# Threshold attention and a bilinear FFN: the score threshold moved from GpSimd to VectorE, the last of seven products added into a free tile, and two tiles for the first batch's tails

## The chip, the cores and the metric

The kernel runs on one core of one Trainium2 chip. The time is device microseconds of one execution, and the median over several executions is what counts. Before the change 13 runs gave a median of 1550.72 us (1540.63 to 1555.79). The engines are called as the profile calls them: PE is TensorE (PEld its weight load), DVE is VectorE, ACT is ScalarE, POOL is GpSimd, SP is SyncE, which here issues nearly all DMAs.

## The reference

```python
# q, k, v: (8, 8, 576, 64); tau = 0.02
scores = matmul(q, k.transpose(0, 1, 3, 2)) / sqrt(64)
thresh = max(scores, axis=-1, keepdims=True) - tau
scores = where(scores >= thresh, scores, -1e9)
attn = exp(scores - max(scores)); attn = attn / (sum(attn) + 1e-9)
x = matmul(attn, v) -> transposed and reshaped to (4608, 512)
a = x @ w_a ; b = x @ w_b          # (512, 1536) each
out = (a * b) @ w_out              # (1536, 512), out is (4608, 512)
```

All is fp32; the weights of the FFN arrive as 64-bit floats and are converted on the chip.

## The kernel before, in words

**Attention.** The work goes by pairs of heads, 32 pairs `i` in 8 batches of 4. Each pair has five units `u`: four of 128 query rows each (two score tiles, one for each head) and one tail with the last 64 rows of both heads (u = NT = 4, one score tile). For one unit, in this order:

- `scores` (L320): PE multiplies q and k into one or two PSUM tiles `sc`; DVE takes the row maximum `mx` (L337); the threshold `thr = mx - cut` is computed on POOL (L340), one instruction for both score tiles; and the bias of the exponential is computed on POOL too (L339) as long as the sums of the FFN weights are not ready (`state["sums"]`), later on ACT (L368).
- `weigh` (L358): ACT computes the exponentials (L369); DVE compares the scores with `thr`, multiplies and sums in one instruction (L372). After it the PSUM tile of the scores is free.
- `reciprocal` and `normalise` (L377, L388): DVE and ACT.
- The weights are transposed. The first 8 units go through PE (`turn_pe`). All others go by 32x32 blocks on DVE (L440, L453), then to a scratch tensor `swap` in DRAM (L448, L460), and `turn_back` (L465) reads them back turned into the tile `wT` (L471). `wT` has one buffer, and `turn_back` issues the next read-back only when `turned` is empty, so only when the one before has been used. In the first batch a pair has three read-backs, h = 0, 1 and the tail h = 2 of its own (128x9x64); later batches have two, the second with the tail in it.
- `weighted` (L577) multiplies `wT` with v (L486, PSUM tile `pv`) and joins the two halves into `x` on ACT and DVE (L475, L476). It runs PV_LAG = 4 units later.

**FFN.** When the four pairs of half a batch are there, POOL copies `x` with its partition halves exchanged into `xS` (L496, eight copies) and, for all blocks but the first, makes four sums of tokens `t` and their exchange `tS` (L547 to L550, L496). There are 18 blocks of 256 tokens. In `ffn` (L604 on) one third of the hidden columns is multiplied directly (`pab`, L632); for the other two thirds, f = 0 and 1, seven products of quarter matrices take the place of eight (`seven`, L702), in the order 1, 6, 2, 5, 7, 3, 4, two products to one PSUM tile. `emptied` (L666) adds each product up in tiles called `kept`, from a ring with the tag "osb" (5 buffers, shared with the output tiles and with the weight conversion): DVE adds (L673 to L688), ACT copies (L671, L678), POOL adds two more (L683, L684) and multiplies the a and b halves into `h` (L664). The last product, m = 4, is added into kept 7 (L688), which POOL also reads at L683. Then `po` multiplies `h` with w_out (L725), and the output tile `osb` is joined and stored.

**What sets the order.** A loop over 160 units (L812) writes all engines' instructions in one order: FFN matmuls are laid between the parts of attention by a pace in columns (`advance`), and `keep_order` fixes the order on each engine as written. Every engine and the SP queue run in that order; an instruction that waits holds up all behind it on its engine. All PSUM tiles are two banks wide and come from one ring of four. The weight conversions, the sums of weights (L517 to L521, POOL) and the first batch fill the first 190 us or so; from then on `state["sums"]` is true.

## Time and profile before

| | us |
|---|---|
| median of 13 runs | 1550.72 (1540.63 to 1555.79) |
| the profiled execution | 1548.07 |
| its span | 1546.3 |
| mean granted PE clock | 0.986 of full speed |
| PE busy | 1441.4 (93%) |
| DVE busy | 921.8 (60%) |
| ACT busy | 656.8 (42%) |
| POOL busy | 495.0 (32%) |

The page gives the busy time of each engine; the chain that ended last, followed back from the last instruction through whatever released each step; and for each group of instructions its count, its busy time, the mean of one, and the idle time of its engine just before it, with what ended that idle time. An "issue" wait is one for which the profile shows no releaser. A wait is put down to the releaser that came last by the profile. Views of a stretch (the waits of one engine, the timeline, the chain in order of time) give the same for a window in microseconds from the start of the span.

### The profile page before, as it was taken

How to read it: one execution, taken by the hardware profiler on the slowest of the kernel's cores; microseconds unless marked ns; L12 is line 12 of the kernel's file. 1: busy time of each engine (PE TensorE's matmuls, PEld its weight loads, DVE VectorE, ACT ScalarE, POOL GpSimd, SP SyncE). 2: the span in 40 equal slices, each digit the busy share in tenths (PEclk: the TensorE clock that was granted, in tenths of full speed). 3: DMA queues.
4: the chain of work that ended last, by engine and by line, in shares of the span. 5: the costliest groups of instructions: out<-in, count | busy, mean ns of one | idle time of the engine just before them, and what ended most of it. 6: DMA issues, size and time to landing. Idle time of an engine off the chain costs nothing.

```text
span 1546.3 us, 65516 instructions
## 1 busy us (share of the span) xinstructions
PE 1441.4 (93%) x29424; PEld 1189.2 (77%) x29424; DVE 921.8 (60%) x1940; ACT 656.8 (42%) x1181; POOL 495.0 (32%) x834
## 2 busy tenths in 40 slices
PE   6778989999999999999999989999999899999998
PEld 4666587786868687879887878778887858798996
DVE  5567667677757776666556756567656766531211
ACT  5666345445444454444343535344534444320000
POOL 3666722221331223122314022312323131413322
PEclk9899999999999999999999999999999999999999
DMA  9657887678767886777555857488757776550000
GB/s 218 156 170 199 168 165 157 161 162 185 175 151 160 178 187 141 160 154 163 133 129 114 185 122 183 95 166 167 182 112 164 156 159 162 112 137 16 4 16 16
DMA packets 625895, 221.81 MB, mean 143 GB/s; under 512 B 543184, under 2 KB 613328, under 8 KB 625616
## 3 DMA queue, kind: packets, MB, share of 16 engines
q1 hardware_dynamic: 623248, 217.04, 63.7%
q8 instruction: 231, 3.78, 1.0%
q10 hardware_dynamic: 2368, 0.59, 0.2%
q14 instruction: 48, 0.39, 0.1%
HBM read 127.40 MB, written 89.65 MB: 140 GB/s over the span
## 4 chain that ended last, share of the span: by engine, by line
PE 85%; DVE 4%; issue 4%; DMA 3%; ACT 2%; POOL 2%; SPq 1%; DVEq 0%; POOLq 0%; ACTq 0%
PE seven L702 26%; PE po L725 24%; PE pab L632 16%; PE pv L486 9%; PE sc L330 9%; DVE mx L337 1%; PE tp L413 1%; DMA wT<-swap 1%; DVE tw L440 1%; DVE tw L372 1%; DMA xS<-xT 1%; DMA kT<-in_k_dram 1%; DVE low L246 1%; DMA sums_u<-in_moe_w_b_dram 0%; ACT tw L369 0%
## 5 line engine op out<-in xcount | busy, mean ns | idle before, releaser
L725 PE MATMUL po<-wo_sb,h 64*64 64x512 f32 x3456 | 415.3, 591 | 1.0 <-POOL h L664 0.6
L725 PEld LDWEIGHTS po<-wo_sb,h 64*64 64x64 f32 x3456 | 235.0, 133 | 119.1 <-issue 67.7
L337 DVE TENSOR_REDUCE mx<-sc 128x1 f32<-128x576 f32 x288 | 205.1, 749 | 162.9 <-PE sc L330 157.4
L330 PE MATMUL sc<-kT,qT 64*64 64x288 f32 x2304 | 238.4, 414 | 23.1 <-DVE kT L318 8.2
L340 POOL TENSOR_SCALAR thr<-mx,scalars 128x2 f32<-128x2 f32 (+1 forms) x160 | 53.6, 335 | 605.6 <-DVE mx L337 605.4
L391 ACT ACTIVATE tw<-tw,rcp 128x576 f32<-128x576 f32 x244 | 176.1, 768 | 136.3 <-DVE rcp L385 136.3
L369 ACT ACTIVATE tw<-sc,bias,scalars 128x576 f32<-128x576 f32 x260 | 215.0, 832 | 32.5 <-POOL bias L339 25.0
L372 DVE SCALAR_TENSOR_TENSOR tw<-sc,thr,tw 128x576 f32<-128x576 f32 x260 | 206.7, 811 | 31.5 <-ACT tw L369 21.1
L486 PE MATMUL pv<-wT,vm 64*64 64x320 f32 (+3 forms) x2592 | 185.5, 382 | 8.0 <-DMA wT<-swap 3.0
L330 PEld LDWEIGHTS sc<-kT,qT 64*64 64x64 f32 x2304 | 141.5, 136 | 65.7 <-issue 26.0
L440 DVE STREAM_TRANSPOSE tw<-tw 128x576 f32<-128x576 f32 x240 | 171.5, 753 | 1.6 <-ACT tw L391 1.5
L486 PEld LDWEIGHTS pv<-wT,vm 64*64 64x64 f32 x2592 | 139.1, 136 | 39.2 <-issue 14.5
L664 POOL TENSOR_TENSOR h<-kept 128x256 f32<-128x256 f32 x136 | 96.6, 730 | 199.9 <-DVE kept L675 150.1
L702 PE MATMUL seven<-tS,sums_u 64*64 64x128 f32 x2176 | 121.2, 271 | 4.7 <-issue 4.7
L702 PE MATMUL seven<-t,sums_u 64*64 64x128 f32 x2176 | 123.0, 271 | 1.1 <-issue 0.9
L368 ACT ACTIVATE bias<-mx,scalars 128x1 f32<-128x1 f32 x252 | 72.2, 287 | 104.6 <-DVE mx L337 104.4
L632 PE MATMUL pab<-xS,wa_sb 64*64 64x256 f32 (+1 forms) x1408 | 102.9, 367 | 8.7 <-POOL xS L496 4.4
L475 ACT COPY xT<-pv 128x256 f32<-128x256 f32 (+1 forms) x68 | 24.5, 360 | 186.5 <-PE pv L486 180.6
L702 PEld LDWEIGHTS seven<-tS,sums_u 64*64 64x64 f32 x2176 | 97.6, 133 | 7.5 <-issue 7.2
L702 PEld LDWEIGHTS seven<-t,sums_u 64*64 64x64 f32 x2176 | 100.5, 133 | 3.5 <-issue 1.8
L476 DVE TENSOR_TENSOR xT<-xT,pv 128x256 f32<-128x256 f32 (+1 forms) x68 | 27.6, 406 | 123.7 <-ACT xT L475 123.7
L632 PE MATMUL pab<-xT,wb_sb 64*64 64x256 f32 (+1 forms) x1280 | 93.9, 363 | 5.5 <-DVE h L640 3.9
(127 smaller groups left out, 2604.0 us busy)
## 6 DMA issues: line engine op xcount, KB each, us to landing
swap<-tw SPq DMA_DIRECT2D x240, 288.0 KB, 5.4
wT<-swap SPq DMA_DIRECT2D x28, 1440.0 KB, 7.8
wT<-swap SPq DMA_DIRECT2D x32, 1152.0 KB, 6.3
vm<-in_v_dram SPq DMA_DIRECT2D x32, 288.0 KB, 4.8
out_dram<-osb SPq DMA_DIRECT2D x32, 256.0 KB, 4.1
qT<-in_q_dram SPq DMA_DIRECT2D x112, 72.0 KB, 3.5
kT<-in_k_dram SPq DMA_DIRECT2D x112, 72.0 KB, 4.8
swap<-wt SPq DMA_DIRECT2D x112, 72.0 KB, 2.9
```

The costliest lines, as they stand in the source:

```text
L330: nc.tensor.matmul(sc[j if u < NT else 0][to, c], qT[r, q0:q0 + D], kT[r, c * SH:(c + 1) * SH], start=True, stop=True)
L337: nc.vector.tensor_reduce(mx[:, c], sc[j], axis=AX.XY, op=ALU.max)
L368: nc.scalar.activation(bias[:, j:j + 1], mx[:, j:j + 1], AF.Copy, scale=e_nscale)
L369: nc.scalar.activation(wb[j], sb[j], AF.Exp, bias=bias[:, j:j + 1], scale=e_scale)
L372: nc.vector.scalar_tensor_tensor(out=wv, in0=sb[j], scalar=thr[:, j:j + 1], in1=wv, op0=ALU.is_ge, op1=ALU.mult, accum_out=sums[:, j:j + 1])
L391: nc.scalar.activation(w, w, AF.Copy, scale=rcp[:, j:j + 1])
L440: nc.vector.transpose(w, w)
L486: nc.tensor.matmul(pv[j * D:(j + 1) * D, r], vm[rows, k0], wT[rows, k0], start=(s == (NT if j == r else 0)), stop=(s == NT - 1))
L632: nc.tensor.matmul(pab[c * D:(c + 1) * D, r], w[rows, f // n, k, fs + c * D:fs + (c + 1) * D], moving, start=(k == 0), stop=(k == H - 1))
L664: pool(hs[f][:, :, c * P:(c + 1) * P], t[:, :, 0], t[:, :, 1], op=ALU.mult)
L702: nc.tensor.matmul(acc[c * D:(c + 1) * D, r, z, y], wq[y][rows, s, e, c * D:(c + 1) * D], xq[s][rows, e], start=(s + e == 0), stop=(s + e ...
L725: nc.tensor.matmul(po[c * D:(c + 1) * D, r], ht[rows, t0:t0 + D], wo_sb[rows, F, :], start=(m == 0), stop=(m == NF - 1))
```

## The change

Three edits. The threshold is computed by DVE once the weight sums are ready, and by POOL before. The last product goes into kept 1, and the ring with the tag "osb" gets a sixth buffer. And the tails' read-backs of the first batch (h = 2) use two tiles in turn: the pairs with an even number take the tag "wt", which else holds a tail's weights in later batches, the others take "wT"; `turn_back` now asks whether the tile that it wants is in use, not whether any is.

```diff
-OSB_BUFS = 5
+OSB_BUFS = 6
...
-        nc.gpsimd.tensor_scalar(thr[:, 0:n], mx[:, 0:n], cut, None, op0=ALU.subtract)
+        engine = nc.vector if state["sums"] else nc.gpsimd
+        engine.tensor_scalar(thr[:, 0:n], mx[:, 0:n], cut, None, op0=ALU.subtract)
...
     def turn_back(g):
 
-        if ready and not turned and ready[0][1] < g:
-            (i, h), _ = ready.pop(0)
+        if not ready or ready[0][1] >= g:
+            return
+        i, h = ready[0][0]
+        tag = "wt" if h == 2 and i % 2 == 0 else "wT"
+        if tag not in [t for t, _ in turned.values()]:
+            ready.pop(0)
             n = width(i, h)
-            wT = work.tile([P, NSLOT, n], FP32, tag="wT", bufs=1, name="wT")
+            wT = work.tile([P, NSLOT, n], FP32, tag=tag, bufs=1, name="wT")
             nc.sync.dma_start(wT, swaps.pop((i, h)).rearrange("(s r) p w -> (r p) s w", r=G))
-            turned[i, h] = wT
+            turned[i, h] = tag, wT
...
                 else:
-                    dve(kept[7], kept[7], acc, op=ALU.add)
-                    times(f2, kept[7], 0)
+                    dve(kept[1], kept[7], acc, op=ALU.add)
+                    times(f2, kept[1], 0)
```

The other changed lines only carry the tag along in `turned`.

## The prediction

> **What bounds the kernel now.** I read the page first: the shares of the engines, then the chain of waits.

> ```profile
> PE 1441.4 (93%) x29424; PEld 1189.2 (77%) x29424; DVE 921.8 (60%) x1940; ACT 656.8 (42%) x1181; POOL 495.0 (32%) x834
> ...
> q8 instruction: 231, 3.78, 1.0%
> ...
> PE 85%; DVE 4%; issue 4%; DMA 3%; ACT 2%; POOL 2%; SPq 1%; DVEq 0%; POOLq 0%; ACTq 0%
> ...
> L340 POOL TENSOR_SCALAR thr<-mx,scalars 128x2 f32<-128x2 f32 (+1 forms) x160 | 53.6, 335 | 605.6 <-DVE mx L337 605.4
> ```

> TensorE (PE) sets the end: it holds 85% of the chain. So an edit is worth only the PE idle time that it takes away. The thr row looks like the prize, 605 us of GpSimd (POOL) waiting at the threshold, but POOL is busy a third of the span; its waiting matters only where PE waits for work queued behind it. Hence the next view: what PE itself waits for, by stage. First the steady stage, 307 to 1400 us:

> ```profile
> PE seven L702 <- issue: 34.9, 31, 3.7
> PE sc L330 <- issue: 7.1, 7, 1.9
> PE pab L632 <- POOL xS L496: 1.2, 1, 1.2
> ```

> Then the turn from the first batch to the second, 160 to 262 us, where the tails are read back:

> ```profile
> PE pv L486 <- DMA wT<-swap: 3.0, 2, 2.1
> ...
> PE pab L632 <- POOL xS L496: 2.4, 1, 2.4
> PE pv L486 <- issue: 1.4, 1, 1.4
> ```

> Columns: total us, times, longest. In 1093 us of steady stage a single 1.2 us wait names POOL; most of what is left is called "issue". The turn holds the waits that the change can reach. After 1400 us the chain is PE without a gap up to the last output tile, so nothing is to be won there.

> **Whether the "issue" waits are in reach.** The chain in order of time around one of them (start, us, what):

> ```profile
> 314.21 1.41 issue
> 315.62 3.72 PE seven L702 x128
> 319.35 0.41 issue
> ```

> PE runs 2 x 29424 = 58848 instructions and queue q8 moves 231 packets, so 255 instructions, or 127 weight-load and matmul pairs, each; the stalls come 128 matmuls apart and in the middle of a product. I take them for the loading of instructions, count them as 0, and keep the other reading as a rival. [...]

> **Tails in two tiles (L465 to L472).** The built programs differ on SP's queue in one place: each of the four 128x9x64 read-backs stands one unit earlier. PE, DVE and ACT keep their order, but for the thresholds on DVE. Before, the fourth is issued at 213.66 and lands 6.8 us later; PE stands still for it (in timeline lines: start, us, instruction, in brackets the idle time before it and what ended it):

> ```profile
> 220.63 1.23 PE L486 MATMUL pv<-wT,vm 64*64 64x64 f32 x34 [2.07 <-DMA wT<-swap]
> ```

> The second costs 0.91 at 203.48. Afterwards the second goes out near 190 and the fourth near 204, the slots of the former first and third, so both land 5 us or more ahead of their product: -0.91 - 2.07 = -3.0 us. Bounds: 0 if the next wait takes over, -3.0 at most, as PE's other waits here are counted below. Queued behind the moved issues on SP are kT, vm and swap issues, each later by one issue (0.4 us); the trace has kT landing over 5 us before its use, so 0. The second tile is the one that the second batch's turns use, first at 319.19. What is late next: the pv at 238.86, which follows.

> **Threshold on DVE (L340), 140 of 160.** The 20 before the weight sums are ready stay on POOL. What POOL loses, 112 x 0.344 + 28 x 0.298 = 47 us, is worth what PE waited for:

> ```profile
> 237.61 0.29 POOL L340 TENSOR_SCALAR thr<-mx,scalars 128x2 f32<-128x2 f32 x1
> ...
> 237.93 0.82 DVE L372 SCALAR_TENSOR_TENSOR tw<-sc,thr,tw 128x576 f32<-128x576 f32 x1 [1.77 <-POOL thr L340]
> ```

> Here thr stood behind two sums and two products on POOL, DVE waited 1.77, the score bank came free at 238.75, and PE's pv, which takes a bank, started at 238.86 after 1.38 idle. That goes: -1.4. Next, the exchange copies:

> ```profile
> 377.07 0.29 POOL L340 TENSOR_SCALAR thr<-mx,scalars 128x2 f32<-128x2 f32 x1 [8.00 <-DVE mx L337]
> 377.42 2.66 POOL L496 COPY xS<-xT 64x256 f32<-64x256 f32 x6
> ```

> Their input was complete at 374.80 (374.38 + 0.42), POOL idle for 8.00 us; they stood behind a threshold that waited for mx. Without it they start 2.6 us earlier. PE feels more than the 1.23 us that its wait shows, since it then runs at the copies' pace: 30 matmuls in 3.9 us, against 1.6 at the 0.054 each of other pab stretches. So -2.6. The same place one block before: input ready at 285.54, copies at 287.66, PE 30 matmuls in 3.6 us: -2.1. At 190.35 the threshold alone lies ahead: -0.35. In the 14 later blocks the copies are done 2.7 us or more ahead of PE: 0. Sum -6.4, between -3.7 (only the waits shown: 0.35 + 1.38 + 0.75 + 1.23) and -6.4.

> The cost on DVE: no row has thr there; the nearest are

> ```profile
> L383 DVE TENSOR_SCALAR sums<-sums 128x2 f32<-128x2 f32 x112 | 20.1, 180 | 0.7
> ```

> and its 128x1 form at 144 ns: 112 x 0.180 + 28 x 0.144 = 24 us, 28 with the step to the next instruction (0.20 from start to start). It stands between mx and the transposes, so those, both weighings, and the kT transpose behind them come up to 0.2 later in each unit. DVE idles 40%, and PE sees it only where it waits for DVE: four scores after a kT transpose (at 359.42, 867.88, 1043.49, 1212.10, gaps 0.4 to 1.2), the product at 523.52, and about three units from 228 to 258: 8 x 0.05 to 0.20. I take 8 x 0.17 = +1.4; the ends are 0 and 28, if every unit paid. [...]

> **Last product into a free tile (L688), sixth buffer.** Now the sum overwrites kept 7, which POOL is still reading at L683:

> ```profile
> L688 DVE TENSOR_TENSOR kept<-kept,seven 128x512 f32<-128x512 f32 x34 | 23.2, 682 | 45.3 <-POOL kept L683 26.8 <-PE seven L702 16.1 <-POOL kept L684 2.4
> ```

> Kept 1 was last read after the third of the seven products, so 26.8 + 2.4 = 29 us of DVE idling goes, which pays for the 24 to 28 us of thr. On PE it shows once, 0.29 at 258.21: -0.3 (0 to -1.5, one such wait). The cover for the rest is PE's own work; were it gone, each of 17 blocks would have paid 1.5. Kept 1 is held longer; the sixth buffer lets the next half's first copy go on, and its other reuses lie a pair of products (over 4 us) back. Conversions show no wait for their buffers: 0.

> **Sum.** -3.0 - 6.4 - 0.3 + 1.4 = -8.3 us. The profiled execution took 1548.07 (span 1546.3): 1539.8. It lies 2.65 under 1550.72, the median of the runs shown, which is what the result is read by; so I subtract from that: **1542.4**.

> **Rivals.** *Handed back in the turn:* the next limit there (DVE, kT's transfers, which the chain names between 200 and 260) takes the 3.0 + 1.38 + 0.35 + 0.3 = 5.0 us, and only the two copies are left: -3.3, 1547.4. For it: from 175 to 275 PE lost about 19 of 100 us (its matmuls priced at the pace of gapless stretches), far more than these waits, so several limits lie close. Against: the waits named are single and nothing else ends near them. *The banks:* the "issue" waits are PE waiting for banks that DVE empties late; a third of 34.9 goes too: about 1531. Against: the 128-matmul spacing. *Slower, DVE's order:* thr delays the kT transpose and the weighing in every unit, and PE, which follows them through banks and kT, pays 0.2 each. It breaks even from 9.7 / 0.2 = 49 of the 140 units; at 80 it is 16 - 9.7 = +6.3: 1557. For it: the four kT gaps. Against: only 8 units show it.

> **How the numbers follow.** Forecast 0.60 (1538.5 to 1546), handed back 0.20, banks 0.08, slower 0.12. A measurement of this kernel tells about 0.3% (4.7 us) from no change: faster 0.68, same 0.20, slower 0.12. The range 1536 to 1551 takes in the forecast with the bounds of its terms and the handed-back case, and leaves out the other two.

> **What would show it.** Right: no PE wait for wT after 200; PE's 30 xS matmuls near 288 and 378 in about 2 us with copies starting right after xT; DVE's L688 row without POOL; DVE busy near 946, POOL near 448; the "issue" waits of seven still near 35. Wrong: scores waiting longer after kT, or PE gaps in the turn with another name. Since those stalls move with the transfers, a few us of them either way would blur a gain this small.

## The result, and the profile after

The changed kernel takes 1539.68 us, the median of 11 runs (1532.15 to 1545.84), against 1550.92 for the kernel before (48 runs, the 13 of above among them). The ratio is 0.9927, 95% interval 0.9909 to 0.9945: 11.3 us faster, 8.5 to 14.1. Forecast were 8.3, which lies just outside that interval. The profiled execution has a span of 1534.3 us, 12.0 under the one before.

The page of the changed kernel, the rows that answer to those shown of before (line numbers after L339 are 1 to 5 higher):

```profile
PE 1430.5 (93%) x29424; PEld 1174.1 (77%) x29424; DVE 952.6 (62%) x2080; ACT 656.6 (43%) x1181; POOL 455.2 (30%) x694
...
q8 instruction: 231, 3.78, 1.0%
...
PE 84%; DVE 5%; issue 4%; DMA 3%; ACT 2%; POOL 1%; SPq 1%; DVEq 0%; ACTq 0%; POOLq 0%
...
L669 POOL TENSOR_TENSOR h<-kept 128x256 f32<-128x256 f32 x136 | 96.5, 728 | 675.6 <-DVE kept L680 431.2
```

POOL idles about as long as before (1079 us against 1051; the row of h now carries the idle time that stood at thr); what changed is what it idles ahead of. What PE waits for, from 307 to 1400 us and then from 160 to 262 us:

```profile
PE seven L707 <- issue: 36.8, 36, 2.8
PE sc L330 <- issue: 5.6, 6, 1.9
```

```profile
PE seven L707 <- issue: 3.0, 2, 1.5
PE pab L637 <- POOL xS L501: 1.6, 1, 1.6
PE pv L491 <- issue: 1.4, 1, 1.4
```

The wait for wT is gone, the waits for xS are gone but for the first, and the "issue" waits of seven are what they were. The wait of pv, which was forecast to go, is there.

Because PE and ACT have the same order in all these kernels, the same instruction can be found in two traces and its start compared. The differences below are those of ACT's copies, in us against the kernel before:

| at (before) | after | tails only | threshold only | free tile only |
|---|---|---|---|---|
| 195.5, ahead of the tails | -0.0 | +1.6 | +0.2 | +1.2 |
| 227.8 | -4.8 | -4.3 | +1.8 | +1.4 |
| 292.0 | -5.3 | -4.2 | +1.7 | +1.4 |
| 300.8, after the second exchange | -8.1 | -4.2 | -1.1 | +2.5 |
| 382.3 | -7.7 | -4.1 | -0.6 | +2.3 |
| 391.0, after the third exchange | -11.8 | -5.5 | -4.7 | +0.9 |
| 406.5 | -8.7 | -4.4 | -0.7 | +1.6 |
| 624.9 | -8.3 | -4.0 | +2.3 | +2.9 |

So by 625 us the trace has just the 8.3 us of the forecast: some five from the turn, three from the second exchange, and four from the third, of which three are handed back within 16 us. That the sum is just 8.3 is luck: the kernel before, profiled a second time (r1 below), is 5.0 us off the first at the same place. The other 3.7 come at "issue" waits and at stretches of half clock (the last section shows one), most of them at 654 to 660 us, where the kernel before has an "issue" wait of 2.86 us with half clock behind it (granted 0.50 from 656.97 us on for 3.41 us). These differed between any two of the profiles.

### The profile page after: what moved, and what is told of

Same layout as the page of the kernel before. It is cut to its first block, busy times and chain, and to the rows that moved or that the text cites. A ratio compares the mean times of both kernels' runs of the same rounds, so it can differ in the third digit from the quotient of the medians.

```text
span 1534.3 us, 65517 instructions
## 1 busy us (share of the span) xinstructions
PE 1430.5 (93%) x29424; PEld 1174.1 (77%) x29424; DVE 952.6 (62%) x2080; ACT 656.6 (43%) x1181; POOL 455.2 (30%) x694
## 3 DMA queue, kind: packets, MB, share of 16 engines
q8 instruction: 231, 3.78, 1.0%
## 4 chain that ended last, share of the span: by engine, by line
PE 84%; DVE 5%; issue 4%; DMA 3%; ACT 2%; POOL 1%; SPq 1%; DVEq 0%; ACTq 0%; POOLq 0%
PE seven L707 27%; PE po L730 23%; PE pab L637 15%; PE pv L491 9%; PE sc L330 9%; DVE mx L337 1%; DVE tw L441 1%; DVE tw L373 1%; DMA xS<-xT 1%; DMA sums_u<-in_moe_w_a_dram 1%; ACT tw L370 0%; DVE low L246 0%; PE tp L414 0%; DMA sums_u<-in_moe_w_b_dram 0%; DMA swap<-tw 0%
## 5 line engine op out<-in xcount | busy, mean ns | idle before, releaser
L730 PEld LDWEIGHTS po<-wo_sb,h 64*64 64x64 f32 x3456 | 229.9, 133 | 124.9 <-issue 73.7
L337 DVE TENSOR_REDUCE mx<-sc 128x1 f32<-128x576 f32 x288 | 205.1, 749 | 151.0 <-PE sc L330 146.3
L330 PE MATMUL sc<-kT,qT 64*64 64x288 f32 x2304 | 234.9, 411 | 23.6 <-DVE kT L318 9.0
L373 DVE SCALAR_TENSOR_TENSOR tw<-sc,thr,tw 128x576 f32<-128x576 f32 x260 | 202.7, 800 | 16.4 <-ACT tw L370 15.9
L330 PEld LDWEIGHTS sc<-kT,qT 64*64 64x64 f32 x2304 | 138.6, 134 | 62.9 <-issue 25.2
L491 PEld LDWEIGHTS pv<-wT,vm 64*64 64x64 f32 x2592 | 139.8, 135 | 37.1 <-issue 11.2
L688 POOL TENSOR_TENSOR kept<-kept 128x512 f32<-128x512 f32 x34 | 43.2, 1271 | 231.2 <-DVE kept L687 187.6
L637 PE MATMUL pab<-xS,wa_sb 64*64 64x256 f32 (+1 forms) x1408 | 98.1, 363 | 7.5 <-DMA xS<-xT 5.9
```

What stands on the lines that cost most here:

```text
L330: nc.tensor.matmul(sc[j if u < NT else 0][to, c], qT[r, q0:q0 + D], kT[r, c * SH:(c + 1) * SH], start=True, stop=True)
L337: nc.vector.tensor_reduce(mx[:, c], sc[j], axis=AX.XY, op=ALU.max)
L373: nc.vector.scalar_tensor_tensor(out=wv, in0=sb[j], scalar=thr[:, j:j + 1], in1=wv, op0=ALU.is_ge, op1=ALU.mult, accum_out=sums[:, j:j + 1])
L491: nc.tensor.matmul(pv[j * D:(j + 1) * D, r], vm[rows, k0], wT[rows, k0], start=(s == (NT if j == r else 0)), stop=(s == NT - 1))
L637: nc.tensor.matmul(pab[c * D:(c + 1) * D, r], w[rows, f // n, k, fs + c * D:fs + (c + 1) * D], moving, start=(k == 0), stop=(k == H - 1))
L730: nc.tensor.matmul(po[c * D:(c + 1) * D, r], ht[rows, t0:t0 + D], wo_sb[rows, F, :], start=(m == 0), stop=(m == NF - 1))
```

## The experiments

Each kernel is named by the label of its run. Ratios are against the kernel before on the same chip (medians 1552.9 to 1554.5 there), the intervals are 95%, and microseconds are worked out from them.

**The edits one by one.** p1 has only `turn_back`; p2 only

```diff
+        engine = nc.vector if state["sums"] else nc.gpsimd
+        engine.tensor_scalar(thr[:, 0:n], mx[:, 0:n], cut, None, op0=ALU.subtract)
```

and p3 only `OSB_BUFS = 6` with kept 1 as the target.

> Only the tails' read-backs in two tiles. Theory (each edit removes PE waits of its own, tails in the turn from batch one to two): PE no longer waits for wT after 200 us, -3 to -5 us against before, all of it gained by the time of 240 us; the copies of xS still wait for the threshold (1.2 us PE wait near 375). Rival (handed back in the turn: the next limit takes it): within 1.5 us of before, with another PE wait of 2 us between 218 and 240.

Measured: 0.9982 (0.9964 to 0.9999), -2.8 us, a little under the expected 3 to 5. After 200 us PE waits for wT no more. Both the wait and the stretch at half clock behind it, worth some 1.4 us more, are gone in the trace (-5.8 from 195 to 228), of which the runs keep about three.

> Only the threshold on DVE. Theory (POOL's copies of xS no longer stand behind a threshold that waits for mx): -5 to -7 us against before, gained at the second and third exchange (near 288 and 377), none of the 0.4 to 1.2 us gaps after kT grows. Rival (DVE's order): the gaps after kT grow by 0.1 to 0.2 us each and the time is -3 us or worse.

Measured: 0.9988 (0.9967 to 1.0010), -1.9 us, less than expected and alone not clear of noise. The gains at the second and third exchange are there; the third is lost again by 402 us. The gaps after kT did not grow: here and in the full change they are 0.75, 1.15, 0.69 and 0.44, as before to the hundredth.

> Only the last product into kept 1, with the sixth buffer. Theory (DVE's 29 us of waits lie beside PE's work): within 1.5 us of before, though DVE's wait for POOL at the last product goes. Rival (DVE empties PSUM banks earlier and PE's waits called issue were waits for banks): -5 us or more, and these waits fall from 35 to under 25 us.

Measured: 0.9976 (0.9960 to 0.9992), -3.7 us. Neither: well over the forecast's 0.3, yet the "issue" waits of seven stay (41.1 us).

**The edits two by two.** q1 is the change without the threshold, q2 without the free tile and sixth buffer, r2 without the tails.

> The changed kernel with every threshold back on POOL: tails in two tiles and the last product into kept 1. Theory (the threshold's own gain at the exchanges is mostly handed back by 410 us; alone it gave 1.4 us): 7 to 10 us under before, that is 1 to 4 us over the changed kernel. Rival (the forecast's sum: the threshold is the largest term, alone it was hidden): 3 to 5 us under before.

Measured: 0.9961 (0.9944 to 0.9978), -6.1 us, between the two expectations.

> The changed kernel without the free tile and the sixth buffer: thresholds on DVE and tails in two tiles. Theory (the free tile's gain is real, 4 us alone, since DVE no longer idles behind POOL at the end of every block): 4 to 7 us under before. Rival (the forecast: the free tile is worth 0.3 us and the 4 us alone are scatter between runs): 9 us or more under before, as the changed kernel.

Measured: 0.9958 (0.9939 to 0.9977), -6.5 us: the theory holds, the free tile is needed for the 11.

> The threshold on DVE and the last product into the free tile with six buffers, the tails as before. Theory (the three edits add up: about -3 for the tails, -3.5 for the threshold, -4 for the free tile): 6 to 9 us under before, PE's wait for wT near 218 still there with its stretch at half clock. Rival (the threshold's cost on DVE is only covered where the tails are early too): 4 us or less under before.

Measured: 0.9931 (0.9903 to 0.9960), -10.7 us, more than expected, with a wide interval. Each edit can thus be seen in four pairs of kernels that differ in it alone: tails -2.8, -2.4, -4.6, -0.6, mean -2.6; threshold -1.9, -3.7, -7.0, -5.2, mean -4.5; free tile with the sixth buffer -3.7, -3.3, -8.8, -4.8, mean -5.2. The pairs mix runs of several chips, each read against the kernel before on its own. A single pair is worth some 3 to 5 us either way and a mean of four some 2, so all three edits gain; that the threshold gains more beside the free tile (-6 against -3) is possible and not shown.

**What in the third edit gains.**

> The kernel before with six buffers in the ring of kept, output and conversion tiles, and nothing else. Theory (a gain of the third edit lies at the last product, not in the ring): within 2 us of before. Rival (the ring held up conversions or output tiles): 3 us or more under before.

Measured: 1.0013 (0.9996 to 1.0029), +2.0 us: the ring alone gains nothing. The free tile without the sixth buffer was not run. r4 doubles the suspected wait instead:

```diff
-                    pool(kept[5], kept[5], kept[7], op=ALU.add)
                     pool(kept[3], kept[3], kept[6], op=ALU.add)
+                    pool(kept[5], kept[5], kept[7], op=ALU.add)
```

> The kernel before with POOL's two additions in the other order, so that the last product on DVE waits for two of them (2.7 us) in place of one (1.4 us) in each block; nothing else. Theory (the free tile gains its 4 us because DVE no longer waits there): 2 to 5 us over before. Rival (that wait lies wholly beside PE's work and the gain comes from elsewhere): within 1.5 us of before.

Measured: 1.0045 (1.0023 to 1.0068), +7.0 us, more than expected. DVE's row for the last product in this kernel, then in the changed one:

```profile
L688 DVE TENSOR_TENSOR kept<-kept,seven 128x512 f32<-128x512 f32 x34 | 23.2, 683 | 71.0 <-POOL kept L684 61.3 <-PE seven L702 9.1 <-POOL h L664 0.7
```

```profile
L693 DVE TENSOR_TENSOR kept<-kept,seven 128x512 f32<-128x512 f32 x34 | 23.0, 677 | 16.2 <-PE seven L707 9.5 <-POOL kept L689 4.8 <-issue 0.9
```

Waiting for POOL's additions there is 29.2 us before (26.8 at L683 and 2.4 at L684), 61.3 with the additions exchanged and 4.8 after. 32 us more of it cost 7 us (3.6 to 10.6), about a fifth; 24 us less gain 4 to 5. Where PE names it, PE is waiting for a bank that DVE has yet to empty. From the fifth block on (459 to 1424 us) PE's waits in r4 include some that the kernel before does not have:

```profile
PE po L725 <- DVE kept L688: 1.7, 2, 1.1
PE sc L330 <- DVE tw L372: 0.5, 1, 0.5
```

and in the turn its scores wait 1.8 us for L688 (0.3 before). That names some 3.7 of the seven us. Where the rest is lost, and where in the trace the free tile's own 4 to 5 us are, stays open: single profiles scatter by as much.

**What the threshold's place in POOL's queue is worth.** In r3 the changed kernel computes the threshold on POOL as well, and nobody reads it:

```diff
+        if state["sums"]:
+            spare = small.tile([P, 2], FP32, tag="spare", name="spare")
+            nc.gpsimd.tensor_scalar(spare[:, 0:n], mx[:, 0:n], cut, None, op0=ALU.subtract)
```

> The changed kernel, in which POOL computes the threshold too, into a spare tile that nobody reads, at the same place as before the change. DVE uses its own. Theory (what the threshold cost was its place in POOL's queue ahead of the exchange copies): the copies near 288 and 377 again start only after mx, PE waits 0.7 to 1.2 us for them again, and the time is that of the changed kernel without its thresholds on DVE, 5 to 7 us under before. Rival (DVE's weighing waited for POOL's answer): the time of the changed kernel, 10 to 12 us under before.

Measured: 0.9939 (0.9920 to 0.9957), -9.5 us, between the two; the time alone decides nothing. The trace does. POOL near the second exchange, first in r3, then in the changed kernel:

```profile
286.71 0.29 POOL L344 TENSOR_SCALAR spare<-mx,scalars 128x2 f32<-128x2 f32 x1 [6.71 <-DVE mx L337]
287.06 3.58 POOL L504 COPY xS<-xT 64x256 f32<-64x256 f32 x8
```

```profile
280.35 0.85 POOL L501 COPY xS<-xT 64x256 f32<-64x256 f32 x2 [12.58 <-DVE xT L481]
281.28 0.73 POOL L552 TENSOR_TENSOR t<-xT 128x256 f32<-128x256 f32 x1
```

With an unread instruction that waits for mx ahead of them, all eight copies come in one go behind it, PE waits again, and the steps of -2.9 and -4.1 at the two exchanges shrink to 0.0 and -1.4. Without it six copies are done before (as each part of x arrives) and the last two follow x at once; PE's matmuls on xS at the second exchange, in the kernel before and in the changed one:

```profile
288.10 3.61 PE L632 MATMUL pab<-xS,wa_sb 64*64 64x256 f32 x30 [0.75 <-POOL xS L496]
```

```profile
281.75 2.10 PE L637 MATMUL pab<-xS,wa_sb 64*64 64x256 f32 x32
```

**The threshold as a sum over a pair.** The long thresholds on DVE were not forecast. In the changed kernel:

```profile
L341 DVE TENSOR_SCALAR thr<-mx,scalars 128x2 f32<-128x2 f32 x112 | 33.0, 295 | 4.0
```

```profile
230.03 1.31 DVE L341 TENSOR_SCALAR thr<-mx,scalars 128x2 f32<-128x2 f32 x1
230.04 1.27 POOL L689 TENSOR_TENSOR kept<-kept 128x512 f32<-128x512 f32 x1
...
231.26 1.43 DVE L441 STREAM_TRANSPOSE tw<-tw 128x576 f32<-128x576 f32 x2
```

The mean is 295 ns, not 180, and of the 140 thresholds all 15 over 0.28 us end within 0.05 us of the end of a POOL instruction that runs beside them. p4 writes the maxima into a tile beside a stored -cut and adds the two:

```diff
-            mx = small.tile([P, 2], FP32, tag="mx", name="mx")
+            pair = pair_of(state); mx = pair[:, :, 0]    # pair[:, :, 1] holds -cut
...
+            nc.vector.tensor_reduce(thr[:, 0:n], pair[:, 0:n], axis=AX.X, op=ALU.add)
```

> The changed kernel with the threshold made on DVE by a sum over the pair (maximum, minus cut) in place of a subtraction with a scalar operand; same order on every engine, two small fills more. Theory (the subtraction on DVE cannot start while a POOL instruction runs: all those above 0.4 us in the changed kernel end with one): no threshold takes over 0.25 us, the one at 230 us shrinks from 1.31 to under 0.25 and PE's 1.42 us wait at 233 goes; time 1 to 2 us under the changed kernel's. Rival (DVE waits for its own maximum or for a semaphore): thresholds of 0.4 to 1.3 us remain at the same places.

```profile
L356 DVE TENSOR_REDUCE thr<-pair 128x2 f32<-128x4 f32 x112 | 17.6, 157 | 3.8
```

Measured: 0.9929 (0.9909 to 0.9949), -11.0 us. The long thresholds are gone, as expected: not one of 140 is over 0.16 us, though 37 run beside POOL, and the same threshold takes 0.16 us with POOL's addition started 0.01 us from it. Near 234 us pv waits 0.2 us for a bank in place of 1.4; but in the other profiles this wait is anything from 0 to 1.6 us, with the threshold on either engine, so one profile does not show why it went. The time is that of the changed kernel, not the 1 to 2 us less that were expected.

**Half of the first exchange on ACT.** q4 is p4 with four of the first eight copies on ACT:

```diff
+                    nc.gpsimd.tensor_copy(xs[0:D, hp], x[D:2 * D, hp])
+                    nc.scalar.copy(xs[D:2 * D, hp], x[0:D, hp])
```

> The threshold by a sum over a pair, and at the first exchange (near 190 us) half of the eight copies on ACT, which idles there. Theory (PE waits 1.6 us there and then runs at the pace of POOL's copies, 30 matmuls in 3.6 us): those 30 matmuls take about 2 us, the time 1 to 3 us under that of the changed kernel, so some 13 us under before. Rival (the next limit takes it, the tails' product or the swap transfers): gained at 196 us, gone by 240 us, time as the changed kernel's.

Measured: 0.9928 (0.9902 to 0.9953), -11.2 us. The 32 matmuls take 1.96 us and the trace is 2.4 us ahead of p4 at 196 us; it is still 4.7 ahead at 301 and only 1.1 at 406. In between:

```profile
388.85 0.83 ACT L387 ACTIVATE tw<-sc,bias,scalars 128x576 f32<-128x576 f32 x1 [4.32 <-DMA swap<-tw]
```

ACT must not write the tile tw before its last contents have gone to swap. The swap issues stand on SP behind four issues of kT that take 6.8 us, so this write-out is the next limit, and a PE that comes earlier waits longer there: ACT 2.24 us in the changed kernel, 4.32 here, with 2.6 us on PE and two stretches at half clock. What the first exchange gains is handed back at 390 us. No version beat the changed kernel.

**The kernel before against itself.**

> The kernel before, unchanged, as a kernel of its own. Theory: a ratio of 1 within 0.2%, which is the scatter that the other runs are read against; its profile differs from the first one by some 3 to 8 us in the instruction-loading waits and in stretches at half clock of 1.7 us each, not in the waits that the change takes away (wT at 203 and 220, the copies near 191, 288, 377). Rival (those waits come and go by chance too): one or more of them missing or twice as long.

Measured: 0.9998 (0.9981 to 1.0016). The waits come again: wT 3.8 us in two, xS 2.5, 0.75 and 1.23; that of pv is 0.8 in place of 1.4.

## Why the prediction was right, step by step

**What bounds.** Right: PE's idle time in the turn and at the early exchanges was where the change worked. The "issue" waits of seven were rightly left out: 34.9 before, 36.8 after, and 29 to 36 from the fifth block to the sixteenth in every profile taken. Of those over 0.2 us from 307 to 1424 us, all 30 before and all 36 after lie on one grid of 127.1 PE matmuls, at the same place in it to within 7%. And in all 66 PE goes on 1.2 to 1.9 us after a packet of q8, the queue of kind "instruction", has ended, which 12% of all its matmuls of that time do. That speaks for the loading of instructions and against banks, which nothing here ties to a count of matmuls.

**Tails, -3.0.** Right in size: mean -2.6 of four pairs. The trace also loses some 1.4 us of half clock that the forecast did not know of.

**Threshold, -6.4 + 1.4 = -5.0.** Right in sum (mean -4.5), wrong in its parts. The exchanges gave -2.9 and -4.1 for the forecast -2.1 and -2.6, and three were handed back where ACT waits for the swap transfer, a limit that no row named before. The wait of pv (-1.4) did not go: on POOL the threshold stood behind the additions, on DVE it waits for the same additions to end (1.31 us at 230.03). It was the step "That goes: -1.4" that failed, and it had read one profile's 1.38 of a wait that is 0 to 1.6 us in others. The price of 180 ns failed too: a threshold with no POOL work beside it takes 0.23 us, and of the 112 with two values 27 run beside POOL, 15 of them for over 0.28 us. Beside POOL one took up to 1.33 us. The cost of +1.4 in the units with a kT gap was 0: in all four the second weighing waits 0.15 us for ACT in the kernel before, and there is no such wait in the changed one.

**Free tile, -0.3.** The mis-sized term, and the step that failed most: about -5 (3.7 alone). The step was "The cover for the rest is PE's own work". It counted the PE waits that name L688 and found one; but 29 us of DVE waiting, in the engine that frees PE's banks, passed on about a fifth to the time, as r4 shows, and only part of it carries its name. DVE's wait for POOL there went from 29.2 us to 4.8, as the forecast had it; what it had wrong is what that is worth. So the total came out near the forecast while its smallest term turned out as large as its largest.

**Rivals.** Handed back in the turn: not there, but it happened at 390 us. The banks behind the "issue" waits: no. DVE's order: no gap after kT grew; the free tile paid for most of it, as forecast (DVE's waits at the last product went from 45.3 to 16.2, its threshold cost 39).

## What to carry to other kernels

An instruction that waits costs what stands behind it in its queue: look at what its engine runs next, not at its own wait (605 us here, worth some five). A wait of an engine that frees PE's buffers can cost time though hardly a PE wait names it (32 us more of it cost 7 here); lengthen it on purpose and see what comes through. And before a gain is counted, look for the next limit further down, 100 us later if need be.

## What the hardware showed that was not expected

**A small subtraction on DVE waited for POOL.** The threshold, a TENSOR_SCALAR from SBUF to SBUF with 2 values per partition, took 0.23 us with POOL idle and up to 1.33 us beside a POOL instruction, until that one ended; TENSOR_REDUCE of the same size took 0.16 at most in all 140. The kernel before has the same: its sums (L383, the row that the price came from) took at most 0.17 us with POOL idle and up to 0.65 beside it. With one value per partition the operation was never long: in the fourteen traces, from 185 us on, 0 of 554 took over 0.28 us, 189 of them beside POOL, against 223 of 2128 with two values, each of which ends within 0.06 us of the end of a POOL instruction. Why the subtraction waits and the sum over a pair does not, no run here shows.

**A short PE wait cost up to 1.7 us more.** The kernel before, by two microseconds (PE busy, then granted clock, DMA share and GB/s), around the wait for the fourth tail:

```profile
218.00:220.00 2.00, 0.44 (x4) 1.00 1.06 170
220.00:222.00 2.00, 1.37 (x46) 0.52 0.37 48
222.00:224.00 2.00, 2.00 (x38) 0.63 0.22 65
224.00:226.00 2.00, 2.00 (x78) 1.00 1.01 334
```

PE waits from 218.56 to 220.63, 2.07 us, and runs at half clock (granted 0.50) from 220.06 on for 3.41 us. With PE busy all through, that is 1.7 us lost; here the first 2.84 us after the wait do the work of 1.42, and 1.4 us more are lost. Between 200 us and the last matmul the kernel before has four such stretches, the changed one none, the threshold alone ten (counting a double one as two), so part of any difference between two profiles is this.
